# Two attention blocks on one core: narrower moment weights, paired denominators, products of zeros in planned gaps, and a retuned plan

## The chip, the cores and the metric

The kernel runs on one core of one Trainium2 chip. The metric is the device time of one execution in microseconds (us), taken over several executions, of which the median is used. TensorE (PE in the profile) multiplies matrices and writes PSUM, VectorE (DVE) and ScalarE (ACT) copy and transform, GpSimd (POOL) sets constants, SyncE (SP) and ScalarE's queue issue transfers (DMAs).

## The reference

Two independent blocks read inputs of 2048 rows by 640, with 32 heads of 20 columns each. Block A is softmax attention, block B is linear attention; their outputs stand side by side.

```python
# A, per head of 20 columns
scores = einsum("bhqd,bhkd->bhqk", q, k) * (Dh ** -0.5)
p = softmax(scores, axis=-1)
o = einsum("bhqk,bhkd->bhqd", p, v)          # then @ wo
# B, per head
phi = lambda t: where(t > 0, t + 1, exp(t)) + 1e-6
pq, pk = phi(q), phi(k)
kv = einsum("bhsd,bhse->bhde", pk, v)
z = einsum("bhsd->bhd", pk)
num = einsum("bhqd,bhde->bhqe", pq, kv)
den = einsum("bhqd,bhd->bhq", pq, z)[..., None] + 1e-6
o = num / den                                # then @ wo
```

## The kernel before, in words

Rows are cut into 16 tiles of 128 and into 4 chunks of 512 (`NQC`, index `tc` or `qc`). Both blocks are worked at once on the one core.

**Block A.** Scores are small for these inputs, so the exponential is replaced by a polynomial of second order in q and k (a guard, `t_guard`, measures whether that is allowed, and otherwise a general path runs). For each key tile, `t_kv` projects K and V, and `t_feat` makes the products of pairs of key columns on VectorE (lines 1372 and 1377, 16 tiles each, into `f_big`). `t_T` (line 1389) sums features times values over all tiles: these are the **moments**. The weights are `Vp`, 32 columns a head of which 20 hold V, one holds ones and 11 hold zeros; four heads go into four column tiles of TensorE, the feature operand has 242 columns, and 16 steps of 32 matmuls add up in four PSUM banks. `t_Tfin` turns the sums into the weight table `Tu`: small selecting matmuls and 24 products with a mask on VectorE (line 1464, the **spreads**), each of which frees the PSUM bank of a selecting matmul. Then come 22 **units** of queries: `t_psi` loads query rows by DMA into one of three slots of `f_big` and multiplies pairs on VectorE (line 1609), `t_pv` multiplies with `Tu` (24 matmuls, the **numerators** and their sums). `t_norm` brings the sums into another layout by DMA, inverts them, brings them back by two more DMAs and multiplies (line 1715), and `t_out` projects with `wo`; the last group's projection of 80 matmuls ends the kernel.

**Block B** (`b_tasks`, line 1810). Keys and values of a chunk are projected, `t_phi` applies phi (exponential on ScalarE, the relu at line 1780 and the sum at line 1803), and key-value products are added up over the four chunks (`kvmm`). For each chunk of queries `qden` projects q, applies phi, and forms the **denominators** (`dmm`, line 2019): five matmuls with 32 weight columns, `kvZ`, and 512 moving columns, into 32 PSUM partitions at `32*tc`. VectorE adds a constant (line 2029), a DMA folds the result into `dc`, VectorE inverts it (line 2038), four DMAs spread it into `Rb`, and `npost` (line 2047) multiplies phi(q) with it. `numout` projects with the combined matrix `Mp`.

**The order of the work.** Nothing is ordered by hand: `_Plan` (line 754) is a list planner that runs when the program is built. Every piece of work is a task with engines, a planned duration, a priority and the tasks that it waits for; a TensorE job also takes a PSUM bank. `step` picks the task that can start first in planned time, by priority among equals, and `run` issues its instructions. So planned durations (for a `job` columns / 2400 + 0.003 us for each entry of `cols`) and the priorities in `_C` fix the order of instructions of each engine, and each engine works through its queue in that order on the chip, with waits on semaphores where data are not there yet. `_WS`, `P1` to `P4` and `_C` are constants of that planner.

## Time and profile before

| | us |
|---|---|
| median of 5 runs | 308.49 |
| lowest, highest run | 306.91, 308.95 |
| the profiled execution | 309.22 |
| its span, first to last instruction | 307.4 |
| mean granted clock of TensorE | 0.983 |

Groups of part 5 of the page that belong to the parts that change (busy time is the union of a group's instructions, the mean is one instruction from start to end; matmuls overlap, so their means are longer than the distance from one to the next):

```profile
L172 PE MATMUL ps<-f_w,f_xT 128*64 128x320 bf16 x640 | 48.6, 307 | 3.1 <-DVE f_xT L1098 2.2
L1377 DVE TENSOR_TENSOR f_big<-f_big 128x3200 bf16<-128x3200 bf16 x16 | 29.1, 1820 | 3.1 <-ACT f_big L1094 3.1
L1609 DVE TENSOR_TENSOR f_big<-f_big 120x1536 bf16<-120x1536 bf16 (+3 forms) x66 | 67.0, 1015 | 4.2 <-DMA f_big<-f_Qd 2.7
```

Each line is: source line, engine, operation, output and inputs with their shapes, how often; then busy us and mean ns of one; then the idle time of that engine just ahead of these instructions and what ended most of it. All matmuls carry line 172, since one helper issues them.

### The profile page before, as it was taken

How to read it: one execution, taken by the hardware profiler on the slowest of the kernel's cores; microseconds unless marked ns; L12 is line 12 of the kernel's file. 1: busy time of each engine (PE TensorE's matmuls, PEld its weight loads, DVE VectorE, ACT ScalarE, POOL GpSimd, SP SyncE). 2: the span in 40 equal slices, each digit the busy share in tenths (PEclk: the TensorE clock that was granted, in tenths of full speed). 3: DMA queues.
4: the chain of work that ended last, by engine and by line, in shares of the span. 5: the costliest groups of instructions: out<-in, count | busy, mean ns of one | idle time of the engine just before them, and what ended most of it. 6: DMA issues, size and time to landing. Idle time of an engine off the chain costs nothing.

```text
span 307.4 us, 8859 instructions
## 1 busy us (share of the span) xinstructions
PE 289.7 (94%) x3807; PEld 193.0 (63%) x3807; DVE 252.3 (82%) x345; ACT 188.3 (61%) x386; POOL 11.5 (4%) x37
## 2 busy tenths in 40 slices
PE   5988999999999997999998899999999889999995
PEld 2766777778565763466666666557554446677873
DVE  6989989999939788977797988999878899994310
ACT  3668788899998772143544256586654475464563
POOL 7200000000000010000000000200000000000000
PEclk9899999999999999599999999999999999999999
DMA  7999565860130337058347736365989979455562
GB/s 250 315 187 188 95 99 92 288 141 9 29 103 20 100 101 220 25 138 209 103 100 220 156 105 179 106 168 117 286 209 185 204 214 229 152 162 176 178 195 94
DMA packets 58745, 47.24 MB, mean 154 GB/s; under 512 B 22994, under 2 KB 57619, under 8 KB 58699
## 3 DMA queue, kind: packets, MB, share of 16 engines
q1 hardware_dynamic: 52443, 38.60, 50.3%
q10 hardware_dynamic: 6256, 8.00, 8.8%
q8 instruction: 32, 0.52, 0.7%
q14 instruction: 14, 0.11, 0.2%
HBM read 30.65 MB, written 11.25 MB: 136 GB/s over the span
## 4 chain that ended last, share of the span: by engine, by line
PE 66%; DVE 13%; DMA 11%; ACT 5%; issue 1%; ACTq 1%; SPq 0%; POOL 0%; DVEq 0%; POOLq 0%
PE ps L172 66%; DMA f_big<-f_Qd 7%; DVE f_big L1609 3%; DVE f_Tu L1464 2%; DMA f_Nd<-f_Rc 2%; DMA f_w<-f_Nd 2%; DVE f_big L1377 2%; DVE f_big L1372 2%; ACT f_big L1094 1%; ACT f_ex L1784 1%; ACT f_pk L1094 1%; ACT f_Ks L1094 1%; DVE f_r L1780 1%; DVE f_pk L1803 1%; ACTq L1689 1%
## 5 line engine op out<-in xcount | busy, mean ns | idle before, releaser
L1609 DVE TENSOR_TENSOR f_big<-f_big 120x1536 bf16<-120x1536 bf16 (+3 forms) x66 | 67.0, 1015 | 4.2 <-DMA f_big<-f_Qd 2.7
L172 PE MATMUL ps<-f_big,f_Tu 120*64 120x512 bf16 (+3 forms) x484 | 54.7, 373 | 3.2 <-DVE f_big L1609 1.6
L172 PE MATMUL ps<-f_w,f_xT 128*64 128x320 bf16 x640 | 48.6, 307 | 3.1 <-DVE f_xT L1098 2.2
L172 PE MATMUL ps<-f_wB,f_xB 128*64 128x320 bf16 x640 | 47.7, 300 | 1.6 <-ACT f_ex L1784 1.0
L172 PEld LDWEIGHTS ps<-f_w,f_xT 128*64 128x64 bf16 x640 | 35.4, 112 | 14.5 <-DVE f_xT L1098 2.3
L172 PEld LDWEIGHTS ps<-f_big,f_Tu 120*64 120x64 bf16 (+1 forms) x484 | 27.5, 109 | 25.7 <-DVE f_big L1609 3.0
L172 PEld LDWEIGHTS ps<-f_wB,f_xB 128*64 128x64 bf16 x640 | 35.8, 110 | 11.0 <-ACT f_ex L1784 1.3
L1094 ACT COPY f_xT<-ps 126x512 f32<-126x512 f32 (+3 forms) x29 | 15.6, 540 | 35.4 <-PE ps L172 32.9
L1094 ACT CAST f_pk<-ps 128x320 bf16<-128x320 f32 (+4 forms) x63 | 25.6, 416 | 10.7 <-PE ps L172 10.3
L1377 DVE TENSOR_TENSOR f_big<-f_big 128x3200 bf16<-128x3200 bf16 x16 | 29.1, 1820 | 3.1 <-ACT f_big L1094 3.1
L1784 ACT ACTIVATE f_ex<-ps 128x320 f32<-128x320 f32 (+1 forms) x52 | 25.2, 500 | 9.7 <-PE ps L172 3.4
L1372 DVE TENSOR_TENSOR f_big<-f_big,f_Ks 128x3200 bf16<-128x3200 bf16 x16 | 29.1, 1820 | 0.0
L172 PE MATMUL ps<-f_xT,f_w 128*64 128x512 bf16 (+3 forms) x240 | 28.1, 404 | 0.0
L172 PE MATMUL ps<-f_wo,f_w 128*64 128x320 bf16 x320 | 23.7, 300 | 0.8 <-ACT f_xT L1094 0.6
L172 PE MATMUL ps<-f_xB,f_wB 128*64 128x512 bf16 x200 | 23.7, 379 | 0.1
L1622 ACT ACTIVATE f_Dq<-f_big 120x512 bf16<-120x512 bf16 (+1 forms) x22 | 13.7, 621 | 14.7 <-DMA f_big<-f_Qd 10.1
L1780 DVE TENSOR_SCALAR f_r<-ps 128x320 f32<-128x320 f32 x32 | 15.1, 488 | 8.4 <-ACT f_ex L1784 7.6
L172 PEld LDWEIGHTS ps<-f_wo,f_w 128*64 128x64 bf16 x320 | 17.5, 110 | 6.5 <-issue 1.4
L172 PEld LDWEIGHTS ps<-f_xT,f_w 128*64 128x64 bf16 (+3 forms) x240 | 12.1, 112 | 12.9 <-issue 4.0
L1094 ACT CAST f_qk<-ps 120x512 bf16<-120x512 f32 (+1 forms) x21 | 12.1, 585 | 12.8 <-PE ps L172 12.7
L1094 ACT CAST f_big<-ps 128x320 bf16<-128x320 f32 (+1 forms) x31 | 13.5, 436 | 8.5 <-PE ps L172 8.4
L172 PEld LDWEIGHTS ps<-f_xB,f_wB 128*64 128x64 bf16 x200 | 11.9, 110 | 9.5 <-ACT f_ex L1784 0.3
(131 smaller groups left out, 369.4 us busy)
## 6 DMA issues: line engine op xcount, KB each, us to landing
f_big<-f_Qd SPq DMA_DIRECT2D x20, 480.0 KB, 5.3
f_big<-f_Qd SPq DMA_DIRECT2D x20, 240.0 KB, 6.5
f_Qd<-f_qk SPq DMA_DIRECT2D x20, 120.0 KB, 1.9
f_Rbc<-f_Nd ACTq DMA_DIRECT2D x3, 720.0 KB
f_w<-f_Nd ACTq DMA_DIRECT2D x4, 480.0 KB
out_dram<-f_pk SPq DMA_DIRECT2D x12, 160.0 KB, 2.1
f_wB<-in_B_wqkv_dram SPq DMA_DIRECT2D x2, 800.0 KB
out_dram<-f_w SPq DMA_DIRECT2D x8, 160.0 KB, 2.8
```

The lines of the kernel that those rows point to most:

```text
L172: lambda e: e.matmul(out, lhsT, rhs, start=start, stop=stop, tile_position=tp, skip_group_check=sgc),
L1094: return self.sch.op("act", lambda e: e.copy(out, in_), reads=reads, writes=writes)
L1372: sch.op("dve", lambda e: e.tensor_tensor(F[:, :, 122:222].rearrange("p h (d a) -> p h d a", a=20), k0.unsqueeze(2).broadcast_to([128, 32, ...
L1377: sch.op("dve", lambda e: e.tensor_tensor(F[:, :, 22:122].rearrange("p h (d a) -> p h d a", a=20), k0.unsqueeze(2).broadcast_to([128, 32, ...
L1464: sch.op("dve", lambda e: e.tensor_tensor(dst.rearrange("p b (v h) -> p b v h", h=nh), src.rearrange("p b (h v) -> p b v h", h=nh), mask.u ...
L1609: sch.op("dve", lambda e: e.tensor_tensor(sl[:, o:o + n, :], sl[:, a:a + 1, :].broadcast_to([120, n, N]), sl[:, b:b + n, :], op=ALU.mult), ...
L1622: sch.op("act", lambda e: e.activation(self.Dq[0:120, dq, 0:N], sl[:, 0, :], AF.Square), reads=(k0,), writes=(("Dq", dq),))
L1689: fn3.append(lambda e, n=n, o=o, i=i, m=m, w=w: e.dma_start(self.Rbc[rb][0:120, i:i + m, 0:w], bass.AP(t.tensor, t.offset + o, [[0, 20], [ ...
L1780: sch.op("dve", lambda e: e.tensor_scalar(r1, ps[:, j.bank, 0:n], 0.0, 1e-6, op0=ALU.max, op1=ALU.add), reads=(("ps", j.bank),), writes=(( ...
L1784: sch.op("act", lambda e: e.activation(ex, ps[:, j.bank, 0:n], AF.Exp), reads=(("ps", j.bank),), writes=(("ex", k, h),))
L1803: sch.op("dve", lambda e: e.scalar_tensor_tensor(dst, self.ex[:, k, 0:m], 1.0, self.r1[:, k, 0:m], op0=ALU.min, op1=ALU.add), reads=tuple( ...
```

## The change

Five things are edited. The moments load 21 of the 32 weight columns in all steps but the first, which still writes the zeros of the other partitions. B's denominators are formed for two chunks in one job, alternately in two column tiles, and the constant's addition and the reciprocal work on both chunks at once. `run` of the planner gets a `fill`: where a TensorE job that takes one bank starts, in planned time, later than TensorE and the bank are free, three quarters of the gap (less 0.2 us) are filled with products of a 128 by 128 block of zeros into that bank. Planned durations of three kinds of job are altered (moments, key-value products, denominators), and the writes of `Tu` are made to wait, in the plan, for two weight permutations whose input they overwrite. All but three of the constants in `_C` have new values. The arithmetic of the result is the same.

```diff
--- before.py
+++ after.py
@@ -765,6 +765,7 @@
         self.open = 0
         self.mode = None
         self.now = 0.0
+        self.fill = None
 
     def add(self, task, deps=()):
         task.seq = self.seq
@@ -872,6 +873,7 @@
         t.start = s0
         if t.acq is not None:
             bk = []
+            x = None
             for pool in t.acq:
                 if pool == "sel2":
                     for x in sorted(self.banks["sel"])[:2]:
@@ -899,6 +901,10 @@
                 tok.remove(x)
                 bk.append(x[1])
             t.bank = bk[0] if len(bk) == 1 else tuple(bk)
+            if e == "pe" and self.fill and len(bk) == 1 and s0 > 12.0:
+                n = int(0.75 * (s0 - max(self.free[e], x[0]) - 0.2) / 0.22)
+                if n > 0:
+                    self.fill(t.bank, n)
         dur = t.durs[t.engs.index(e)]
         if e == "pe" and t.mode is not None:
             if t.mode != self.mode:
@@ -944,8 +950,9 @@
 P3 = (0.0, 0.4)
 P4 = (0.0, 0.6)
 _WS = 176
-_C = dict(q=0.62, qs=0.04, ks=0.0, kd=-0.005, bk=8.07, bks=0.0, bq=-3.62, bo=0.169, out=1.37, pv=0.0, fe=4.51,
-          psi=7.74, r=-3.6, f=-1.2, nm=0.91, op=4.0, kv=3.3, npo=0.1, bqs=0.0013, bd=0.0, bn=3.56)
+_C = dict(q=1.22, qs=0.002, ks=-0.005, kd=0.002, bk=8.14, bks=0.02, bq=-1.65, bo=0.169, out=0.65, pv=0.05,
+          fe=5.19, psi=8.0, r=-3.73, f=-3.51, nm=-0.06, op=5.55, kv=5.2, npo=0.04, bqs=0.0013, bd=0.0,
+          bn=3.21)
 
 
 class _Fast:
@@ -1395,12 +1402,13 @@
             for g in range(N_GRP):
                 for i in range(4):
                     h = 4 * g + i
-                    sch.mm(ps[32 * i:32 * i + 32, g // 2, 256 * (g % 2):256 * (g % 2) + 242], self.Vp[:, s2, h, :],
+                    w = 21 if t else 32
+                    sch.mm(ps[32 * i:32 * i + w, g // 2, 256 * (g % 2):256 * (g % 2) + 242], self.Vp[:, s2, h, 0:w],
                            self.F[:, s, h, 0:242], start=(t == 0 and g % 2 == 0), stop=(t == self.NT - 1),
                            reads=(("Vp", s2, h // 16), "Vp0", ("F1", s)) + keys,
                            writes=(("ps", g // 2),), tp=(0, 32 * i), inc=(g == N_GRP - 1 and i == 3), sgc=True)
             yield
-        return self.job(mms, [293] * N_GRP, deps, prio=0.5, pool=None)
+        return self.job(mms, [245] * N_GRP, deps, prio=0.5, pool=None)
 
     def t_Tfin(self, last):
 
@@ -1481,7 +1489,7 @@
                     sch.barrier(("dve",), ("w0r", "w0B"))
                 spread(self.Tu[0:m, x, 0:4, :], ps[0:m, j.bank, 0:504].rearrange("p (b w) -> p b w", b=4),
                        self.M6[0:m], m)
-            done.append(self.dve(0.68, post, (j,), prio=0.2, rel=(("aux", j),)))
+            done.append(self.dve(0.68, post, (j, self.ew[0], self.ewB[0]), prio=0.2, rel=(("aux", j),)))
         for q in range(6):
             def mms(b, q=q):
                 for y in range(2):
@@ -1501,7 +1509,7 @@
                 for y in range(2):
                     m = 120 if q + y else 123
                     spread(self.Tu[0:m, 2 * q + y, 4:6, :], v[0:m, 2 * y:2 * y + 2, :], self.M6[0:m], m)
-            done.append(self.dve(0.84, post, (j,), prio=0.2, rel=(("aux", j),)))
+            done.append(self.dve(0.84, post, (j, self.ew[0], self.ewB[0]), prio=0.2, rel=(("aux", j),)))
         done = [plan.add(_Task("none", 0.0, lambda t: None), done)]
         self.ones = []
         for s in range(self.NS):
@@ -1811,7 +1819,7 @@
         sch, ps = self.sch, self.ps
         NQC = self.NQC
         kvprev = (start,)
-        kvlast, kvx, dcl = [], {}, {}
+        kvlast, kvx, dcl = [], {}, []
         PB, BK = _C["bq"], _C["bk"]
 
         def va1(_):
@@ -1855,7 +1863,7 @@
                                     writes=(("ps", b),), inc=(c == cs[-1] and tl == 3), sgc=True)
                             one = False
                     yield
-                j = self.job(kvmm, [290] * (4 * len(cs)), ks + vs, prio=_C["kv"])
+                j = self.job(kvmm, [185] * (4 * len(cs)), ks + vs, prio=_C["kv"])
                 kvprev.append(j)
 
                 def kvpost(_, j=j, cs=cs, tc=tc):
@@ -2014,41 +2022,49 @@
                 qj.append(j)
                 qs.append(self.t_phi([j], 512, pqT[:, c, :], ("pqT", tc, c), fr, fw, eps=False))
             qall[tc] = self.plan.add(_Task("none", 0.0, lambda t: None), qj)
-            pr = slice(32 * tc, 32 * tc + 32)
+            return qs
+
+        def den(k, qs):
+
+            tcs = (2 * k, 2 * k + 1)
+            pr = slice(64 * k, 64 * k + 64)
 
             def dmm(b):
                 for c in range(N_DC):
-                    sch.mm(ps[pr, b, :], self.kvZ[:, c, :], pqT[:, c, :], start=(c == 0), stop=(c == N_DC - 1),
-                           reads=("kvZ", ("pqT", tc, c)), writes=(("ps", b),), tp=(0, 32 * tc),
-                           inc=(c == N_DC - 1))
+                    for tc in tcs:
+                        sch.mm(ps[32 * tc:32 * tc + 32, b, :], self.kvZ[:, c, :], pqs[tc][:, c, :], start=(c == 0),
+                               stop=(c == N_DC - 1), reads=("kvZ", ("pqT", tc, c)), writes=(("ps", b),), tp=(0, 32 * tc),
+                               inc=(c == N_DC - 1 and tc % 2 == 1), sgc=True)
                 yield
-            j = self.job(dmm, [590] * 5, qs + [zf], prio=_C["bd"])
-
-            def dpost(_, j=j):
+            j = self.job(dmm, [540] * 5, qs + [zf], prio=_C["bd"])
+
+            def dpost(_):
                 sch.barrier(("dve",), tuple(("mask", c) for c in range(N_DC)) + ("mask0",))
                 sch.op("dve", lambda e: e.tensor_scalar(self.dn[pr, :], ps[pr, j.bank, :], self.cn[pr, 0:1], 1e-6,
                                                         op0=ALU.add, op1=ALU.add),
-                       reads=(("ps", j.bank), "cn"), writes=(("dn", tc),))
-            e1 = self.dve(0.62, dpost, (j, cn), prio=1.0, rel=(("aux", j),))
-            dc = self.dc[:, tc % 2, :]
-            m1 = self.spd([lambda e: e.dma_start(dc, self.dn[pr, :].rearrange("h (j q) -> h j q", j=4))],
-                          (e1, dcl.get(tc - 2)), (("dn", tc),), (("dc", tc % 2),), prio=0.5, q="act", lat=6.0)
+                       reads=(("ps", j.bank), "cn"), writes=(("dn", k),))
+            e1 = self.dve(0.7, dpost, (j, cn), prio=1.0, rel=(("aux", j),))
+            m1 = self.spd([lambda e, tc=tc: e.dma_start(
+                self.dc[:, tc % 2, :], self.dn[32 * tc:32 * tc + 32, :].rearrange("h (j q) -> h j q", j=4)) for tc in tcs],
+                [e1] + dcl[-2:], (("dn", k),), ("dc",), prio=0.5, q="act", lat=4.5)
 
             def rc(_):
-                sch.op("dve", lambda e: e.reciprocal(dc, dc), reads=(("dc", tc % 2),), writes=(("dc", tc % 2),))
-            e2 = self.dve(1.1, rc, (m1,), prio=0.9)
-            k = tc % 2
-            m2 = self.spd([lambda e, i=i: e.dma_start(self.Rb[32 * i:32 * i + 32, k, :].rearrange("h (j q) -> h j q", j=4), dc)
-                           for i in range(4)],
-                          (e2, bar, rbprev.get(tc - 2)), (("dc", tc % 2),), (("Rb", k),), prio=0.5, lat=5.0)
-            dcl[tc] = m2
-
-            def npost(_):
-                sch.op("dve", lambda e: e.scalar_tensor_tensor(
-                    pqT, pqT, 1e-6, self.Rb[:, k, :].unsqueeze(1).broadcast_to([128, N_DC, 512]), op0=ALU.add,
-                    op1=ALU.mult), reads=(("Rb", k),), writes=tuple(("pqT", tc, c) for c in range(N_DC)))
-            rbprev[tc] = self.dve(2.9, npost, (m2,), prio=_C["npo"])
-            return rbprev[tc]
+                sch.op("dve", lambda e: e.reciprocal(self.dc[:], self.dc[:]), reads=("dc",), writes=("dc",))
+            e2 = self.dve(1.9, rc, (m1,), prio=0.9)
+            res = []
+            for tc in tcs:
+                m2 = self.spd([lambda e, i=i, tc=tc: e.dma_start(
+                    self.Rb[32 * i:32 * i + 32, tc % 2, :].rearrange("h (j q) -> h j q", j=4), self.dc[:, tc % 2, :])
+                    for i in range(4)], (e2, bar, rbprev.get(tc - 2)), ("dc",), (("Rb", tc % 2),), prio=0.5, lat=5.0)
+                dcl.append(m2)
+
+                def npost(_, tc=tc):
+                    sch.op("dve", lambda e: e.scalar_tensor_tensor(
+                        pqs[tc], pqs[tc], 1e-6, self.Rb[:, tc % 2, :].unsqueeze(1).broadcast_to([128, N_DC, 512]),
+                        op0=ALU.add, op1=ALU.mult), reads=(("Rb", tc % 2),), writes=tuple(("pqT", tc, c) for c in range(N_DC)))
+                rbprev[tc] = self.dve(2.9, npost, (m2,), prio=_C["npo"])
+                res.append(rbprev[tc])
+            return res
 
         def numout(tc, nm):
             pqT = pqs[tc]
@@ -2075,11 +2091,11 @@
                     self.out[128 * t:128 * (t + 1), D_MODEL:2 * D_MODEL], self.stB[sg - 4])],
                     evs, (("st", sg, 0), ("st", sg, 1)), (("bout", t),), lat=6.5)
 
-        held = []
+        nms = []
+        for k in range(NQC // 2):
+            nms += den(k, qden(2 * k) + qden(2 * k + 1))
         for tc in range(NQC):
-            held.append((tc, qden(tc)))
-        for x in held:
-            numout(*x)
+            numout(tc, nms[tc])
 
 
 
@@ -2142,6 +2158,13 @@
             self.ex_[tc] = plan.add(_Task("none", 0.0, lambda t: None), (self.ext[tc][0], self.ext[tc][3]))
         xn_free = [self.ex_[0], self.ex_[1]]
         cdone = self.cdone = self.mid_consts()
+
+        def fill(b, n):
+
+            mv = self.zt[:].unsqueeze(1).broadcast_to([128, 4, 128])
+            for _ in range(n):
+                sch.mm(ps[:, b, :], self.zt[:], mv, start=True, stop=True, reads=("zt",), writes=(("ps", b),), sgc=True)
+        plan.fill = fill
 
         TP, kns, feats, vqs = [], [], [], []
         for t in range(NT):
```

## The prediction

> **What bounds the kernel now.** I read the page first (parts 1, 2 and 4), then the busy time by stretches of 10 us, then TensorE's own waits, then TensorE's timeline around the places that the diff touches. The page gives the frame.
>
> ```profile
> span 307.4 us, 8859 instructions
> PE 289.7 (94%) x3807; PEld 193.0 (63%) x3807; DVE 252.3 (82%) x345; ACT 188.3 (61%) x386; POOL 11.5 (4%) x37
> PEclk9899999999999999599999999999999999999999
> PE 66%; DVE 13%; DMA 11%; ACT 5%; issue 1%; ACTq 1%; SPq 0%; POOL 0%; DVEq 0%; POOLq 0%
> ```
>
> TensorE (PE) is busy 289.7 of 307.4 us, idle 17.7. It is the bound, and a microsecond of its queue is worth about a microsecond if the next thing it waits for is ready. One slice has half clock. The chain of waits agrees: 66% on TensorE. The stretches show where the 17.7 us are, and where VectorE (DVE) is nearly as full.
>
> ```profile
> 20.00:30.00 10.00, 8.96 (x164) 6.60 (x160) 8.32 (x10) 8.19 (x16) 0.00 (x0) 1.00 0.97 199
> 30.00:80.00 50.00, 49.56 (x890) 38.67 (x888) 47.66 (x49) 43.69 (x88) 0.00 (x0) 1.00 0.53 115
> 80.00:110.00 30.00, 30.00 (x431) 18.86 (x428) 23.15 (x26) 25.60 (x45) 0.00 (x0) 1.00 0.25 72
> 126.00:127.00 1.00, 1.00 (x8) 0.36 (x4) 0.93 (x3) 0.00 (x0) 0.00 (x0) 0.50 0.00 0
> 150.00:180.00 30.00, 27.57 (x376) 19.79 (x374) 25.56 (x41) 13.94 (x34) 0.00 (x0) 1.00 0.62 161
> 240.00:250.00 10.00, 7.85 (x80) 4.11 (x78) 8.90 (x12) 5.61 (x12) 0.00 (x0) 1.00 0.77 199
> ```
>
> Columns: stretch, PE, weight loads, DVE, ACT, POOL, clock, DMA. Idle of TensorE: about 5.5 us in the first 30, nearly nothing from 30 to 110 (the moments), some 2 around 120, 5.4 between 150 and 250 (the numerators), 3.8 after its last matmul. From 30 to 80 VectorE is at 95% too; from 80 to 110 only at 77%. In one-microsecond stretches the clock is 0.50 from 123.7 to 130.1. The timeline gives the prices of what is changed, and the end of the kernel:
>
> ```profile
> 55.43 1.01 PE L172 MATMUL ps<-f_big,f_Vp 128*32 128x242 bf16 x32
> 56.37 2.91 PE L172 MATMUL ps<-f_w,f_xT 128*64 128x320 bf16 x40
> ...
> 220.40 1.25 PE L172 MATMUL ps<-f_pq,f_kvZ 128*32 128x512 bf16 x5
> 221.58 2.57 PE L172 MATMUL ps<-f_big,f_Tu 123*64 123x512 bf16 x22
> ...
> 275.87 2.54 PE L172 MATMUL ps<-f_big,f_Tu 123*64 123x512 bf16 x22
> 278.25 0.38 PE L172 MATMUL ps<-f_Dq,f_Tu 120*64 120x512 bf16 x2
> ...
> 297.99 5.62 PE L172 MATMUL ps<-f_wo,f_w 128*64 128x320 bf16 x80 [0.17 <-DVE f_w L1715]
> ```
>
> Start to start, a moments step takes 0.94 us and a denominator job 1.18. After the last numerator ends (278.6), TensorE fills 19.4 us with projections while that numerator is copied, inverted and scattered by DMAs; the last 80 matmuls wait only 0.17 us for it.
>
> **What the Trainium skill says.** "TensorE: Matmul & The Clock Gate", section "LDWEIGHTS (loading the stationary operand)": the load's time goes by its columns, columns / 1.2 ns. The trace: 32 loads of 32 columns took 0.74 us, 23.1 ns each, a little under its 26.7. The same page, "What's actually happening": the clock is halved after an idle window and comes back after about 3.4 us of activity. The trace has one such stretch, 6.4 us, though TensorE never stood for more than 0.28 us at a time there; it was thinly used. "TensorEngine Tiling (Array Packing)", "Theoretical Speedup": operands of 64 columns or less run up to 2 at once in column tiles. The trace has it: ten 512-column matmuls of 64 columns go in 1.08 us, 0.216 a pair. The same page, "Key Properties": changing the tiling mode drains the array; no row of this trace isolates that cost.
>
> **The change part by part.** *Moments.* Each of 16 steps has 8 groups of four (load, matmul) pairs; 0.94/8 = 117 ns a group. Loads alone, from the page: 4 x 26.7 = 107 ns with 32 columns, 70 with 21 (estimate). Streaming alone, from the 320-column pairs (0.140 us a pair): 242/320 x 0.140 = 0.106. With 21 columns streaming is the floor: 8 x 0.106 = 0.85 us. 15 steps change (the first keeps 32), so the gain is between 0 and 15 x 0.09 = 1.4; I take 1.3.
>
> *Denominators.* Before, 4 x 1.18 = 4.72 us. After, two jobs of five pairs, 2 x 5 x 0.216 = 2.16 (if they overlapped not at all: 4.72). I take -2.5; bounds -2.6 and 0. VectorE gains too: four additions of 744 ns become two, 1.5 us, and the reciprocal stays about the same (four of 916 ns against two of twice the columns). Against it: the chain dn, DMA, reciprocal, DMA, product now waits for both chunks. In the new order of instructions 22 us of TensorE work stand between the second pair of denominators and the first numerators of chunk 2, and the old landings were 5.8 and 6.8 us (f_wB<-f_dc, f_dc<-f_dn), so I cost it at nothing; if the cover failed, about 3 us.
>
> *Products of zeros.* The new order holds 11: 3 early, 1 ahead of a numerator, 1 near the end, 6 ahead of the last 80 matmuls. One is 512 columns, 0.216 us at full clock. The early 3 fall where TensorE idles anyway (1.04 us between 20 and 30). The last 6 fill a gap that the planner thinks at least 0.2 + 6 x 0.22/0.75 = 1.96 us long. I don't see that gap: from the last numerator to the last 80 the new order has 290 projection matmuls at 0.070, 20.3 us, and some 0.6 of small work, against a chain that took 19.4. So 8 are pure addition, 1.7 us, and four switches of mode at the planner's 0.105 add 0.4: +2.1; bounds 0 (all in real gaps) and +2.8. None of the 11 stands in the stretch of half clock: there the matmuls wait for a free bank, and the fill begins only once the bank is free. So that stays.
>
> *Planner figures alone.* The two jobs of B's key-value products (40 matmuls) were planned at 20 x 0.124 = 2.48 us; they took 1.59, from 190.53 to 192.12, and the new figure gives 1.60. With the retuned constants and the two added dependencies of the Tu writes this moves the whole order. Up to the last moments step the new order has 80 fewer matmuls of B's keys and values (80 x 0.070 = 5.6) and 60 fewer of A's queries (6 x 1.08 = 6.5); with the moments' 1.3 that is 13.4 us less for TensorE, so its last moments step could start at 110.3 - 13.4 = 97. VectorE up to the last feature product: 96.6 us of work in the first 110.2, less 4 relus (0.41 each), one 640-wide sum (0.74), four copies (0.4) and the two guard reductions: about 91.5. With the 4.4 us it loses at the start between 0 and 30 and the 4.7% it idles from 30 to 80, it ends at about 98 to 99. So in the moments both engines are now full; TensorE waits 1.5 us more for features, and 12 us of its work move to where VectorE has time. From the Tu spreads on, VectorE has the same work as before in a stretch some 10 us longer. What it left late, part of the 5.4 us between 150 and 250, should shrink; bounds -4 and +2, as loads there land only after 10.6 to 12 us (chain of waits, 219 to 246) and don't care for VectorE. I take -2.4. After them the first thing late is again the numerators' slots.
>
> Sum: -1.3 - 2.5 + 2.1 + 1.5 - 2.4 = -2.6. The profiled execution took 309.22 us (span 307.4 and 1.8 around it): 306.6. The median shown is 0.73 lower, so 305.9.
>
> **The rivals.** *A, slower: the moments go at VectorE's pace.* If VectorE's idle time up to the last product stays at 110.2 - 96.6 = 13.6 us, since features wait for ACT copies that wait for TensorE, the last step starts at 91.5 + 13.6 = 105 and TensorE has nothing ready: 8 us of waits in place of 1.5, so 305.9 + 6.5 = 312.4. It turns slower by over 0.5% once the last step starts later than about 101.5. For it: VectorE at 95% from 30 to 80. Against: most of that idle (6.9 us) lies in 80 to 110, where TensorE alone was full, and at the start. *B, no change: the later stalls stay.* They are waits for loads, not for VectorE; with -2.4 gone, 308.3. For it: those 10 to 12 us landings. *C, more than forecast:* the fills fall in real gaps (-2.1) and the moments add no wait (-1.5): 302.3. For it: the planner's figures now agree with the trace for several kinds of job. That the change doesn't do what it says applies to its fills alone, and is in the sum.
>
> **How the numbers follow.** Forecast 0.48 (302.8 to 307.5), A 0.24, B 0.16, C 0.12. About 0.5% (1.5 us) is what a measurement of this kernel can tell from no change. Faster: forecast and C, 0.60; same: B, 0.16; slower: A, 0.24. The range goes from 301.5 to 311: it holds the forecast, B, most of C and half of A. The likeliest case's own range is the one given with its chance.
>
> **What would show it.** Moments step at 0.85 us start to start; the pair of denominators at 1.1; the last moments step at 97 to 101; one stretch of clock 0.50 of about 6 us after the spreads; last 80 matmuls after six zero products with no wait in between; TensorE idle in the numerators below 4 us. Wrong if TensorE idles before moments steps for over 5 us, or the half clock comes twice.

## The result and the profile after

The changed kernel takes 310.29 us (median of 42 runs, 307.3 to 312.76), the kernel before beside it 308.41 (79 runs, 306.16 to 311.75): a ratio of 1.0063, 95% interval 1.0048 to 1.0077. A ratio leaves out executions that took over 1.5% longer than the fastest of the same kernel; medians and extremes hold all. The prediction was 305.9 and faster; the change made the kernel slower by 1.9 us. The profiled execution took 309.8 us with a span of 307.9, against 309.22 and 307.4: these two differ by 0.6 us only, so the stretches below show where time went in one execution each and don't add up to the 1.9.

The page of the changed kernel, its head and the shares of its chain of waits:

```profile
span 307.9 us, 8876 instructions
PE 289.2 (94%) x3818; PEld 192.9 (63%) x3818; DVE 250.6 (81%) x340; ACT 188.0 (61%) x387; POOL 11.5 (4%) x37
PEclk9799999999999998999999999999999979999999
PE 70%; DVE 13%; DMA 9%; ACT 3%; issue 1%; SPq 1%; ACTq 0%; POOL 0%; POOLq 0%; DVEq 0%
```

TensorE is busy 0.5 us less than before and idle 18.7 us in place of 17.7. Of its clock (the digits of `PEclk`, tenths of full speed in 40 slices of the span), the 5 of before (the slice from 123) has become an 8 (from 115), but a 7 has appeared further on (from 246). Busy time by stretches of the span (columns: stretch, length, PE, weight loads, DVE, ACT, POOL, clock, DMA share, GB/s) shows where the idle time went:

```profile
30.00:110.00 80.00, 78.72 (x1296) 56.33 (x1292) 74.91 (x86) 69.21 (x132) 0.99 (x2) 1.00 0.43 98
230.00:262.00 32.00, 26.73 (x288) 15.91 (x286) 25.05 (x24) 15.55 (x33) 0.00 (x0) 0.95 0.73 185
```

TensorE's idle time, length less busy time, stretch by stretch:

| stretch, us | before | after |
|---|---|---|
| 0 to 30 | 5.48 | 4.27 |
| 30 to 110 (moments) | 0.44 | 1.28 |
| 110 to 130 (spreads) | 2.21 | 1.75 |
| 130 to 230 | 3.33 | 1.95 |
| 230 to 262 | 2.25 | 5.27 |
| 262 to the end | 3.95 | 4.20 |

Everything up to 230 improved by 2.2 us in sum, and 3.0 were lost between 230 and 262. TensorE's timeline there (start, length from first start to last end, then the instructions; in brackets the idle time ahead of them and what ended it):

```profile
234.94 3.56 PE L172 MATMUL ps<-f_wo,f_w 128*64 128x320 bf16 x50
241.09 2.56 PE L172 MATMUL ps<-f_big,f_Tu 123*64 123x512 bf16 x22 [2.59 <-DVE f_big L1617]
...
251.30 1.54 PE L172 MATMUL ps<-f_pk,f_pq 128*64 128x320 bf16 x10 [2.69 <-DVE f_pq L2062]
252.64 1.98 PE L172 MATMUL ps<-f_xB,f_wB 128*64 128x512 bf16 x10
```

Two waits, 2.59 us for products of query rows and 2.69 for B's phi(q) times its inverted denominators; then the clock is halved for 3.4 us (250.7 to 254.1): ten 320-column matmuls take 1.54 us, elsewhere 0.85 to 0.87, ten of 512 columns 1.98, elsewhere 1.25. VectorE's timeline of the same stretch gives the reason for both:

```profile
232.91 0.74 DVE L1702 RECIPROCAL f_Rc<-f_Rc 96x96 f32<-96x96 f32 x1
236.22 1.75 DVE L2052 RECIPROCAL f_dc<-f_dc 128x256 f32<-128x256 f32 x1 [2.57 <-DMA f_dc<-f_dn]
237.89 3.15 DVE L1617 TENSOR_TENSOR f_big<-f_big 120x2048 bf16<-120x2048 bf16 x3
...
248.42 2.83 DVE L2062 SCALAR_TENSOR_TENSOR f_pq<-f_pq,f_wB 128x2560 bf16<-128x2560 bf16 x1 [2.86 <-DMA f_wB<-f_dc]
```

VectorE stands still for 2.57 us at the first pair's reciprocal, whose operand comes by DMA. Behind it in the same queue are the products for TensorE's next numerators (line 1617, unit 17), whose query rows had landed by 233.4 (ScalarE squared them then). They start only at 237.89, and TensorE waits at 241.09. The second standstill is at B's product, line 2062. In the kernel before, VectorE came to the first two reciprocals 11 us after ScalarE's queue issued their DMAs (239.76), and did not stand there:

```profile
250.85 1.76 DVE L2038 RECIPROCAL f_dc<-f_dc 128x128 f32<-128x128 f32 x2
```

The two waits share the loss differently from one execution to the next. In those of e1 (the changed kernel without the zeros) and e2 (with 32 weight columns throughout), both below and otherwise in the same order, the first wait was 2.47 and 3.42 us, the half clock came right behind it (the 22 matmuls took 4.09 and 3.96 us), and the second wait was 0.22 and 0.40.

### The profile page after: what moved, and what is told of

Read it like the earlier page. It is cut to its first block, busy times and chain, and to the rows that moved or that the text cites. A ratio compares the mean times of both kernels' runs of the same rounds, so it can differ in the third digit from the quotient of the medians.

```text
span 307.9 us, 8876 instructions
## 1 busy us (share of the span) xinstructions
PE 289.2 (94%) x3818; PEld 192.9 (63%) x3818; DVE 250.6 (81%) x340; ACT 188.0 (61%) x387; POOL 11.5 (4%) x37
## 4 chain that ended last, share of the span: by engine, by line
PE 70%; DVE 13%; DMA 9%; ACT 3%; issue 1%; SPq 1%; ACTq 0%; POOL 0%; POOLq 0%; DVEq 0%
PE ps L172 70%; DMA f_big<-f_Qd 3%; DMA f_dc<-f_dn 3%; DMA f_wB<-f_dc 3%; DVE f_Tu L1472 2%; DVE f_big L1384 2%; DVE f_big L1379 2%; DVE f_big L1617 1%; DVE f_pq L2062 1%; DVE f_pq L1284 1%; ACT f_ex L1792 1%; SPq L2056 1%; DVE f_dc L2052 1%; DVE f_dn L1286 1%; ACT f_pk L1101 1%
## 5 line engine op out<-in xcount | busy, mean ns | idle before, releaser
L172 PE MATMUL ps<-f_big,f_Tu 120*64 120x512 bf16 (+4 forms) x484 | 54.6, 373 | 3.4 <-DVE f_big L1617 2.6
L172 PEld LDWEIGHTS ps<-f_big,f_Tu 120*64 120x64 bf16 (+2 forms) x484 | 26.9, 109 | 25.4 <-DVE f_big L1617 3.3
L172 PEld LDWEIGHTS ps<-f_wB,f_xB 128*64 128x64 bf16 x640 | 36.5, 110 | 8.3 <-issue 1.1
L1792 ACT ACTIVATE f_ex<-ps 128x320 f32<-128x320 f32 (+1 forms) x52 | 25.6, 499 | 10.4 <-PE ps L172 8.6
L172 PE MATMUL ps<-f_xT,f_w 128*64 128x512 bf16 (+2 forms) x240 | 26.5, 389 | 0.0
L172 PE MATMUL ps<-f_xB,f_wB 128*64 128x512 bf16 x200 | 24.4, 387 | 0.0
L1101 ACT CAST f_big<-ps 128x320 bf16<-128x320 f32 (+1 forms) x33 | 14.2, 435 | 9.6 <-PE ps L172 9.3
L172 PEld LDWEIGHTS ps<-f_xT,f_w 128*64 128x64 bf16 (+2 forms) x240 | 11.9, 108 | 11.1 <-issue 1.0
L1797 ACT ACTIVATE f_r<-ps 128x512 f32<-128x512 f32 x20 | 11.9, 596 | 10.4 <-PE ps L172 8.5
```

The lines of the kernel that those rows point to most:

```text
L172: lambda e: e.matmul(out, lhsT, rhs, start=start, stop=stop, tile_position=tp, skip_group_check=sgc),
L1101: return self.sch.op("act", lambda e: e.copy(out, in_), reads=reads, writes=writes)
L1792: sch.op("act", lambda e: e.activation(ex, ps[:, j.bank, 0:n], AF.Exp), reads=(("ps", j.bank),), writes=(("ex", k, h),))
L1797: sch.op("act", lambda e: e.activation(r1, ps[:, j.bank, 0:n], AF.Relu), **rw)
```

## The experiments

Ratios are to the kernel before, run on the same chip in the same period. The intervals don't hold what differs between chips: one order of instructions, run twice on two chips (e10 and e15 below), gave 1.0095 and 1.0036, another (e5 and e13) 0.9928 and 0.9949.

**Zeros and weight columns taken back.** e1 is the changed kernel with `plan.fill = None`, e2 has `w = 32` in all steps.

> The changed kernel with the same plan, but the 11 products of zeros are not issued; all else is in the same order. Theory: the eight after 190 us stand on TensorE's path (1.40 us ahead of the last 80 matmuls, 0.46 ahead of a numerator, 0.3 near the end), so the median falls from 310.3 by 1.5 to 2.5 us, to about 308.3, and the last 80 matmuls start about 2 us earlier. Rival: they keep the clock up or fill waits that are there anyway; then the time stays within 0.5 us of 310.3 or rises, and a further stretch of clock 0.50 shows.

> The changed kernel with 32 weight columns in all moments steps, the plan unaltered. Theory: the width of the weights does not set the pace of a step, which stays at 0.94 us start to start, and the time stays within 0.5 us of 310.3. Rival (the prediction's reading): loads of 21 columns are faster and the gain is only hidden by waits for features; then steps take longer than those of the changed kernel, and the time rises by up to 1.4 us, to 311.7.

e1: 309.24 us, ratio 1.0034 (1.0009 to 1.0058). The zeros cost about 0.9 us (1.0063 less 1.0034, times 308; the intervals just overlap), so at most half of the loss: 1.0 us of it stays without them. e2: 309.97, ratio 1.0065 (1.0032 to 1.0098), the same as the changed kernel within the intervals: 21 or 32 weight columns make no difference that shows.

**What a moments step costs.** The widths are changed in pairs of steps. e8 leaves out part of the computation: columns of V or of the features in eight of the 16 steps.

```diff
-                    w = 21 if t else 32
+                    w, nf = {3: (32, 242), 4: (32, 242), 5: (8, 242), 6: (8, 242), 7: (21, 121), 8: (21, 121),
+                             9: (32, 121), 10: (32, 121), 11: (21, 32), 12: (21, 32)}.get(t, (21 if t else 32, 242))
...
```

> The changed kernel with other shapes in some moments steps (so the sums of those steps leave out parts of V or of the features): steps 3, 4: 32 weight columns and 242 moving columns; 5, 6: 8 and 242; 7, 8: 21 and 121; 9, 10: 32 and 121; 11, 12: 21 and 32; the others 21 and 242. Start to start, now 0.94 us. Theory: a pair of load and matmul costs 29.4 ns whatever the widths, so all steps stay within 0.05 us of 0.94. Rival S (streaming bounds): steps with 121 moving columns fall to 0.45 to 0.55 us. Rival L (loads bound): step time goes with the weight columns, 8 columns well below 21.

TensorE's timeline of that kernel, two steps and what follows each (128*8 is 128 rows by 8 weight columns; 128x242 the moving operand):

```profile
44.17 1.00 PE L172 MATMUL ps<-f_big,f_Vp 128*8 128x242 bf16 x32
45.11 0.60 PE L172 MATMUL ps<-f_w,f_xT 128*64 128x320 bf16 x6
...
59.89 0.61 PE L172 MATMUL ps<-f_big,f_Vp 128*21 128x121 bf16 x32
60.43 0.46 PE L172 MATMUL ps<-f_w,f_xT 128*64 128x320 bf16 x4
```

Start to start a step takes 0.94 us with 8 weight columns, as with 21 and 32, and 0.54 with half the moving columns (0.53 to 0.54 with 32 weight columns too); with 32 moving columns it took 0.30. Per group of four matmuls that is 117, 67 and 37 ns: 0.41 ns a moving column between the first two, and some 17 ns that don't go by columns (some 24 at 32 columns). My theory, that each pair of load and matmul has a price of its own whatever the widths, fell; the rival, that the streaming of the moving columns sets the pace, stands. The Trainium skill ("TensorE: Matmul & The Clock Gate", "Measured speedup vs the span model") gives a pack of tiles the time of one matmul plus some 4 ns for each further tile; that is 12 ns for four tiles, as an estimate, where e8 has 17.

**Is the second wait a matter of where B's first projection stands?** e3 makes chunk 0's projection wait, in the plan, for the second pair's denominators (`hold` in its list); e4 is e3 without zeros.

> The changed kernel, with one edit to the plan: B's projections of chunk 0 may be planned only after the second pair of denominators, so that the first of them no longer stands in TensorE's queue ahead of the last ten query matmuls and a numerator. Theory: the 2.7 us wait for phi(q) times the inverse and the stretch of half clock after it (about 1.4 us lost) go, and the median falls by 3 to 4 us, to about 306.8. Rival: the queue then waits at the next numerator or at the slots' loads instead, the gain is below 1 us, and a wait of over 2 us shows within 10 us of the old place.

> Both edits at once: the held projection and no products of zeros. Theory: the two costs stand in different places of TensorE's queue and add up: 310.3 - 3.5 - 2 = about 304.8, faster than both kernels. Rival: the end of the kernel is then set by the last group's chain of DMAs (its product ended 0.26 us before TensorE came to the zeros), so that only one of the two gains is kept, about 306.8.

e3: 309.91, ratio 1.0025 (1.0001 to 1.0049); e4: 308.86, 1.002 (0.9993 to 1.0048). The wait ahead of B's projection went, but the wait ahead of the numerators grew to 3.54 us, and its 22 matmuls then took 4.90 us in place of 2.56: the loss had another place to go.

**Is it the reciprocal's place?** e5, without zeros, lets the reciprocal of the first pair wait, in the plan, for unit 17's products.

```diff
-            e2 = self.dve(1.9, rc, (m1,), prio=0.9)
+            e2 = self.dve(1.9, rc, (m1, self.pd[17] if k == 0 else None), prio=0.9)
```

> The changed kernel without products of zeros, and with one more dependency in the plan: the reciprocal of the first pair of denominators waits for the pair products of unit 17, so that on VectorE it stands behind them and not ahead of them. (The planner then also places B's first projections later.) Theory: in the changed kernel the reciprocal stands in VectorE's queue while its DMA takes 9.4 us where 4.5 were planned; the products behind it, whose rows landed at 233.4, start only at 237.9, and TensorE waits 2.6 us for them, with half clock after it in some executions. With the order turned round that wait falls below 0.8 us, VectorE's wait for f_dc<-f_dn falls below 1 us, and against the kernel without zeros (309.2) the median falls by 2.5 to 3.5 us, to about 306.3. Rival: the rows of the unit are what is late, as loads take 7 to 12 us there; then the wait of about 2.5 us stays and the time stays within 1 us of 309.2.

305.98 us, ratio 0.9928 (0.9902 to 0.9953): faster than both kernels. In VectorE's timeline of e5 the products now come first and the reciprocal stands 0.69 us:

```profile
233.87 3.21 DVE L1617 TENSOR_TENSOR f_big<-f_big 120x2048 bf16<-120x2048 bf16 x3 [0.54 <-DMA f_big<-f_Qd]
237.76 1.75 DVE L2053 RECIPROCAL f_dc<-f_dc 128x256 f32<-128x256 f32 x1 [0.69 <-DMA f_dc<-f_dn]
```

Between 230 and 262 TensorE is busy 31.32 of 32 us (26.73 in the changed kernel). I took this for proof that the place of one instruction was the loss. But a new dependency lets the planner place everything behind it anew, and the next runs show that more had moved.

**The halves of the change alone.** e6 is the kernel before with the new constants, the new durations of moments and key-value products, and the `Tu` dependencies; e7 is the kernel before with the paired denominators only, the planned landings of their DMAs among them.

> The kernel before with only the retuned constants, the planner's new figures and the two added dependencies: 32 weight columns, denominators chunk by chunk, no products of zeros. Theory: the new order by itself costs nothing (VectorE is fuller in the moments, TensorE idles no more), the reciprocals stand late enough in VectorE's queue, and the median is within 1 us of 308.2. Rival A: the new order itself is what is slow, with TensorE waiting for features; then the last moments step starts later than 99 us and the median is over 309.7. Rival B: the order is better, as predicted: 306.5 or less.

> The kernel before with only the paired denominators; constants and all other figures as before. TensorE has 2.4 us less work. Theory: the pair's reciprocal stands again in VectorE's queue ahead of a unit's products, its DMA lands late, TensorE waits 2 us or more before a numerator between 235 and 255, and the gain is spent: the median is within 1 us of 308.2. Rival: the harm needs the retuned order; then there is no such wait and the median falls by 2 us or more, to 306.2.

e6: 309.94, ratio 1.0053 (1.0032 to 1.0074). e7: 310.98, ratio 1.0073 (1.0044 to 1.0102). Each loses alone. e6 has no large wait, but many small ones between 230 and 262 (3.84 us idle, before 2.25) and 1.47 idle in the moments (before 0.44); I did not trace them further. Its last moments step starts at 97.35, so it isn't the prediction's rival A, which had it at 105. e7 has the pattern of the changed kernel: the pair's reciprocal stands 2.94 us for its DMA ahead of products, and TensorE waits 1.69 for those.

**The same dependency elsewhere, and on the whole change.** e9 is e7 with e5's dependency, e10 the whole change, zeros too, with it.

> Kernel before with the pairs of denominators alone, and the one dependency more: the first pair's reciprocal waits for unit 17's products. Theory (the pairs hurt because the shared reciprocal waits for its DMA at the head of VectorE's queue, ahead of products whose rows have landed): the wait of 1.69 us ahead of the numerators near 244 is gone or under 0.5, the reciprocal follows its wait by under 1 us, and the kernel is at 306.0 to 307.5 against 308.3 for before. Rival (the pairs hurt through their late second half, where VectorE ends later and the last 80 matmuls wait for it; the dependency only moves the order): still 308.5 or more, with the last 80 matmuls waiting 1 us or more. The new order also puts the first pair some 40 us earlier, so a miss with neither wait would mean that the rest of the order decides.

> The whole change, products of zeros among it, with that one dependency. The planner now puts 20 products of zeros ahead of the last 80 matmuls, where it saw 6, and one ahead of B's last 80. Theory: the two waits of 2.6 and 2.7 us and the half clock between 251 and 254 are gone (-5 or so), and the 20 zeros (4.3 us) take the place of a wait of 2.76 us there and add about 1.5 to 2: 307 to 308.5, 1.5 to 2.5 slower than the same kernel without zeros. Rival (zeros keep the clock up and cost nothing, being in a real gap): equal to the kernel without zeros, 306.

e9: 312.0, ratio 1.0128 (1.0087 to 1.0169), a miss. The wait it aimed at is gone and the first pair's denominators stand where they stood (226.08 us, in e7 226.34), but the order behind them changed and other waits came (1.11 us ahead of an output projection, 1.06 ahead of numerators, 1.35 ahead of the last 80 matmuls). Which of them costs the time was not tried. e10: 310.35, ratio 1.0095 (1.0062 to 1.0128): the two waits and the half clock are gone as expected, and the planner had put 20 zeros ahead of the last 80 matmuls; the time was above the range I gave.

**One exchange and nothing else.** e5 changed more than one place. So in e11 only two entries of VectorE's queue are exchanged after planning (the reciprocal is issued right behind unit 17's products; all other engines keep their order); e12 does that to e3.

```diff
-                sch.op("dve", lambda e: e.reciprocal(self.dc[:], self.dc[:]), reads=("dc",), writes=("dc",))
+                def op():
+                    sch.op("dve", lambda e: e.reciprocal(self.dc[:], self.dc[:]), reads=("dc",), writes=("dc",))
+                if k == 0:
+                    self.kept.append(op)
+                else:
+                    op()
...
             mul(1, 0, 1, 3, (k0, k2), (("sl", s, "C"), k2))
+            if self.kept:
+                self.kept.pop()()
```

> The changed kernel with two instructions' places exchanged and nothing else: the first pair's reciprocal is written behind unit 17's three products on VectorE; every other engine has the same order. Theory (two stalls share one chain: dn, DMA, reciprocal, DMA, product, first B projection): the wait of 2.59 us ahead of the numerator near 241 is gone, so TensorE reaches B's first projection 2.6 us earlier; but its inputs come 0 to 1 us later than before, so the wait there grows from 2.69 to between 5 and 6.5 us and the time stays, 309.8 to 311.5 (ratio 1.004 to 1.010). Rival (the reciprocal's place alone is the loss): the first wait goes, the second grows by under 1 us, and the time falls by 2 to 3, to 307.3 to 308.3 (ratio 0.997 to 1.000).

> The kernel with B's first projection held behind the second pair's denominators, and the same exchange of places on VectorE and nothing else. Theory (each of the two is enough to keep the loss, so they have to go together): the wait of 3.54 us ahead of the numerator near 243 and its half clock (4.90 for 22 matmuls, 2.54 at full clock) both go, and no wait over 1 us takes their place between 235 and 262; of the 5.9 us at that place 2 or more may come back as waits for the last group's chain at the end, so 304.5 to 307 (ratio 0.987 to 0.996, against 1.0025 without the exchange). Rival (the chain of loads behind sets the pace, and the waits only move): the time stays at 308.5 or more, and waits of the same sum stand later.

e11: 313.16, ratio 1.0155 (1.0108 to 1.0203). The direction is the theory's, the size beyond it. TensorE's timeline of e11:

```profile
247.34 0.61 PE L172 MATMUL ps<-f_Dq,f_GW 120*32 120x512 bf16 x6
254.14 1.54 PE L172 MATMUL ps<-f_pk,f_pq 128*64 128x320 bf16 x10 [6.19 <-DVE f_pq L2069]
255.48 2.34 PE L172 MATMUL ps<-f_xB,f_wB 128*64 128x512 bf16 x10
257.61 3.29 PE L172 MATMUL ps<-f_big,f_Tu 123*62 123x512 bf16 x22
```

The first wait has shrunk to nothing and the second has grown from 2.69 to 6.19 us, with a longer stretch of half clock behind it (6.8 us in place of 3.4). The reciprocal itself now runs 2.8 us later (239.01 in place of 236.22), and B's product with it (251.26 in place of 248.42). e12: 311.44, ratio 1.01 (1.0053 to 1.0148): my theory, that both waits go if both places are mended, fell. VectorE's timeline of e12 shows why:

```profile
250.84 2.83 DVE L2070 SCALAR_TENSOR_TENSOR f_pq<-f_pq,f_wB 128x2560 bf16<-128x2560 bf16 x1 [6.58 <-DMA f_wB<-f_dc]
253.58 1.48 DVE L1813 SCALAR_TENSOR_TENSOR f_xB<-f_ex,f_r 128x512 bf16<-128x512 f32 x2
...
257.71 0.69 DVE L1813 SCALAR_TENSOR_TENSOR f_xB<-f_ex,f_r 128x512 bf16<-128x512 f32 x1
```

VectorE stands 6.58 us at B's product for its second DMA, and behind it in the queue is phi of the last chunk's queries (line 1813), which the second pair's denominators need: TensorE waits 3.46 us there, for an exponential on ScalarE, whose queue had itself stood 5.94 us for line 1813, and 1.62 us for line 1813 itself. The queue is held by the same chain, one step further on. So it isn't the place of one instruction alone: my next theory was that the whole chain of the pair comes later than the plan has it, and that what is placed around it pays.

**The planned landing.** The planner counts 0.55 us to issue each DMA on ScalarE's queue and then `lat` until the data are there. The diff lowers `lat` of the sums' DMA from 6.0 to 4.5, an edit that the list of changes above does not name: planned 0.55 + 6.0 = 6.55 us before, where the trace of before has 6.8 from issue to landing (the last figure; the query counts the first two of the four DMAs):

```profile
f_dc<-f_dn ACTq DMA_DIRECT2D x2, 64.0 KB, 6.8
```

In the changed kernel it is 2 x 0.55 + 4.5 = 5.6 us from the first of the pair's two issues. That issue stood at 226.16 and the reciprocal could start at 236.22, 10.1 us later. Its chain of waits, from the second issue on:

```profile
226.82 9.38 DMA f_dc<-f_dn
236.22 1.76 DVE f_dc L2052
238.00 0.62 SPq L2056
...
239.95 8.44 DMA f_wB<-f_dc
248.42 2.84 DVE f_pq L2062
```

The second transfer is planned at 4 x 0.5 + 5.0 = 7.0 us from its first issue and took 10.4 (238.00 to 248.42). Over the two the chain is 7.9 us later than planned (4.5 and 3.4). e13 puts back 6.0 and nothing else, e14 sets both nearer the trace (8.0 and 7.0, so 9.1 and 9.0 planned), both without zeros; e15 is e13 with zeros; e16 gives e7 the figures of e14.

```diff
-                [e1] + dcl[-2:], (("dn", k),), ("dc",), prio=0.5, q="act", lat=4.5)
+                [e1] + dcl[-2:], (("dn", k),), ("dc",), prio=0.5, q="act", lat=8.0)
...
-                    for i in range(4)], (e2, bar, rbprev.get(tc - 2)), ("dc",), (("Rb", tc % 2),), prio=0.5, lat=5.0)
+                    for i in range(4)], (e2, bar, rbprev.get(tc - 2)), ("dc",), (("Rb", tc % 2),), prio=0.5, lat=7.0)
```

> The changed kernel without products of zeros, and one figure put back to what it was before the change: the planned landing of the sums' DMAs (dn to dc), 6.0 in place of 4.5. Theory (the planner believed the pair's sums would land early and put the reciprocal, B's products and B's first projection too early on three engines): the waits of 2.5 and 2.7 us in front of the numerator near 241 and of B's first projection go, and the time is that of the kernel with the reciprocal behind unit 17's products: ratio to before 0.989 to 0.996. Rival (the gain of that kernel was particular to its chip or its run): 1.000 or more.

> As the run before, with both landings of B's chain as the trace has them: 8.0 for dn to dc, 7.0 for dc to the multipliers. Theory: no wait for the reciprocal or for B's products; the same as the run before within 0.5%, since its order differs from it only after 262 (three products of the last group on VectorE, ScalarE's copies), 0.986 to 0.996. Rival: the later part gets worse, 1.000 or more, with a wait of more than 3 us before the last 80 matmuls.

> The changed kernel with the planned landing 6.0 in place of 4.5 and with its products of zeros (27, 20 of them ahead of the last 80 matmuls). Against the same without zeros on this chip: theory (they stand in a gap of 2.8 us and take 4.4; the six and one before add 1.3): 2 to 3 us slower, ratio to before 0.998 to 1.004. Rival (zeros cost more than their time, as two comparisons on different chips suggest): 4.5 to 5.5 slower, 1.006 to 1.012.

> The kernel before with the pairs alone and both landings as the trace has them (8.0 and 7.0). Theory (the pairs lose only by the early plan of their chain): better than with 4.5 and 5.0, which had 1.0073: 0.995 to 1.002. Rival (in this order the pairs bring other waits, as with the dependency alone, which had 1.0128): 1.007 or more, with waits of over 1 us ahead of an output projection or the last 80 matmuls.

All four ran on one chip, where before took 307.87:

| kernel | us | ratio | interval |
|---|---|---|---|
| e13, 6.0 and 5.0, no zeros | 306.47 | 0.9949 | 0.9926 to 0.9973 |
| e14, 8.0 and 7.0, no zeros | 302.77 | 0.9835 | 0.9783 to 0.9886 |
| e15, 6.0 and 5.0, with zeros | 309.48 | 1.0036 | 1.0017 to 1.0056 |
| e16, pairs alone, 8.0 and 7.0 | 309.53 | 1.0018 | 0.9986 to 1.0051 |

e13 has on every engine the order of e5, so what that dependency did, the one number does. Between 230 and 262 TensorE stands 1.35 us in e13, 5.27 in the changed kernel. Against e1 (1.0034) the number is worth 0.85% or 2.6 us; e1 ran on another chip, so the size is good only to the 0.2 to 0.6% by which one order differed between chips, but both chips that ran the order of e13 have it faster than before. e14 is the best kernel of the study, 5.1 us below before (six executions), and better than I expected; I had expected e13 and e14 equal. Between them only the end differs. VectorE's timeline of e13, near the end:

```profile
281.08 2.83 DVE L2062 SCALAR_TENSOR_TENSOR f_xB<-f_xB,f_wB 128x2560 bf16<-128x2560 bf16 x1 [3.56 <-DMA f_wB<-f_dc]
283.83 1.75 DVE L1723 TENSOR_TENSOR f_w<-f_xT,f_Rbc 120x1536 bf16<-120x1536 f32 x1
285.50 0.54 DVE L1702 RECIPROCAL f_Rc<-f_Rc 96x64 f32<-96x64 f32 x1
...
294.08 1.23 DVE L1723 TENSOR_TENSOR f_w<-f_xT,f_w 120x1024 bf16<-120x1024 f32 x1 [6.36 <-DMA f_w<-f_Nd]
```

and of e14:

```profile
273.95 0.55 DVE L1702 RECIPROCAL f_Rc<-f_Rc 96x64 f32<-96x64 f32 x1 [2.48 <-DMA f_Rc<-f_xT]
274.42 2.76 DVE L2062 SCALAR_TENSOR_TENSOR f_xB<-f_xB,f_wB 128x2560 bf16<-128x2560 bf16 x1
...
287.42 1.22 DVE L1723 TENSOR_TENSOR f_w<-f_xT,f_w 120x1024 bf16<-120x1024 f32 x1 [0.75 <-DMA f_w<-f_Nd]
```

With the later figures the planner puts block A's last reciprocal ahead of B's products, at 273.95 in place of 285.50, and the last product that the final 80 matmuls need comes at 287.42 in place of 294.08. In e13 those 80 wait 2.37 us; in e14 they follow without a wait, at 291.77. It is the same fault, at the second pair.

e15 is 3.0 us slower than e13 on the same chip: the planner's fill grows from 11 products of zeros to 31, most of them at the end. TensorE's timeline of e15:

```profile
293.00 4.49 PE L172 MATMUL ps<-f_zt 128*128 128x512 bf16 x20
297.42 5.62 PE L172 MATMUL ps<-f_wo,f_w 128*64 128x320 bf16 x80
```

Twenty zeros take 4.4 us where e13 waits 2.37 and e5 2.76, and the six and one ahead of B's last projection add some 1.3. So with the zeros the better figure brings no clear gain (1.0036 and 1.0095 in e15 and e10, against 1.0063).

e16 leaves the pairs alone open. Its ratio, 1.0018 where e7 on another chip had 1.0073, holds nine executions; the other six took 312.5 to 315.8 us, and none of the 51 of before took more than 310.4. The profiled execution is one of the six: VectorE no longer stands at the reciprocal, but TensorE waits 1.20 us ahead of an output projection and 2.97 ahead of numerators, waits like those that the rival named. In that order of work the landings alone don't explain the loss.

## Why the prediction was wrong, by its own steps

- **The step that failed**: "the chain dn, DMA, reciprocal, DMA, product now waits for both chunks ... so I cost it at nothing; if the cover failed, about 3 us". I looked at TensorE work ahead of the second pair's use, and took the old landings (5.8 and 6.8). I did not look at the first pair, at what stands behind its reciprocal in VectorE's queue, or at the figure 4.5 in the diff against the 6.8 in the trace of before. The runs showed in its place two waits, 5.3 us, and 1.4 us of half clock (0.67 and 0.73 over full clock). e13 puts the one figure at about 2.6 us, and e14, with both figures nearer the trace, lies 5.1 us below before; both were run without zeros. The cost of "if the cover failed", about 3 us, was of the right size: it was left out of the sum.
- **Moments, -1.3**: 0. A step stayed at 0.94. I scaled the 320-column pair (0.140 us, two tiles) by its columns to 106 ns. e8 has some 17 ns in each group of four tiles that columns don't shorten, and a group took 117 ns: streaming was the bound with 32 weight columns already.
- **Denominators, -2.5**: right. The first pair's job goes from 222.87 to 224.05, 1.18 us, so 2.4 for two in place of 4.72.
- **Zeros, +2.1**: about 0.9 (e1 against the changed kernel); more where the planner is told a later landing (3.0, e15 against e13, 31 zeros). The six ahead of the last 80 have no wait behind them, as said.
- **Waits in the moments, +1.5**: 0.84 (1.28 idle in place of 0.44). The last step started at 97.49, in the forecast's 97 to 101, in part by luck: the moments gave none of their 1.3, but TensorE idled 1.2 us less in the first 30 (4.27 in place of 5.48), which no term held. Rival A, the moments at VectorE's pace, did not occur: the kernel is slower, but for another reason.
- **Later waits, -2.4**: -1.4 up to 230, and +3.0 from 230 to 262, where the prediction said "after them the first thing late is again the numerators' slots". It was the query products behind a reciprocal, and B's own product.
- **Half clock**: I said that it would stay, and read it as 6.4 us; the clock of before has 6.8 (123.3 to 130.2). After the change it lasted 3.4 us (114.2 to 117.6), worth at most 1.7 us. That is not the change's doing: in e1, with the same order, it lasted 3.4 us, in e2 6.8. And it came a second time, which the prediction named as the sign that it was wrong.

## What to carry to other kernels

When a change merges two transfers into one chain, look at what is queued behind the instruction that waits for it on its own engine, not only at the time until its result is used; and where a planner orders the work, compare each latency that the change gives it with the landing in the trace (here 5.6 against 10.1 us) before anything else. "Issue the DMA early, do compute, wait on its semaphore late" (the Trainium skill, "DMA: Bandwidth & Descriptors", "Rules for kernel authors") paid here only where the plan knew how late: with the zeros left out, both figures set nearer the trace turned 0.3% slower (e1) into 1.65% faster (e14), on two chips. A gain from a new dependency is no proof of the reason for it: exchange the two instructions alone before you believe it.

## What the runs showed of the hardware that was not expected

- A DMA of 64 KB from one layout of the on-chip memory to another (`f_dc<-f_dn`) took 6.8 us from issue to landing before, 9.4 in the changed kernel and 9.5 in e5, while the DMA engines were busy for 0.87 of the time (before) and all of it (the other two), at 190 to 204 GB/s. The same DMA took 2.1 us in e7 for the second pair (from 265.8, the engines busy for 0.40 of the time) and 2.4 us for the last chunk of before (from 271.8, busy for 0.80). The Trainium skill ("DMA: Bandwidth & Descriptors", "Anatomy of one DMA") fits about 2.0 us plus bytes / 436e3 for another way of issuing, 2.15 us for 64 KB as an estimate: near the 2.1 and 2.4, far from the 9.4, and the measurement decides. So most of the landing near 230 us looks like queueing behind other transfers, for which the busy share is a rough sign only; whose, was not tried.
- The clock of TensorE halved at 250.7 after a wait of 2.69 us, but not after the 2.59 at 241, nor in e5 after 2.76 ahead of its last 80 matmuls (5.62 us). In the profiled execution of e13, with the order of e5, it halved after 2.37, and the last 80 took 7.30: that is why its profiled time (308.33) is above its median. The length of the wait doesn't decide it; how the wait falls on a grid agrees with all of these. In all 18 traces the clock changes only at whole multiples of 3.41 us from its first change. Cut on that grid, the changed kernel's stretch from 237.04 has TensorE busy for 0.43 of it, and full clock follows; that from 247.28 has 0.39, and half clock follows. In e13 one stretch holds the wait (busy 0.30), in e5 two share it (0.66 and 0.53). Between 30 and 300 us of the 18 traces, all 11 full-clock stretches with TensorE busy for 0.40 or less are followed by half clock, and none of the three between 0.43 and 0.58 is. After the spreads half clock follows at 0.59 to 0.67 too, which other places pass at full clock; what differs there stays open.
- A moments step took 0.94 us with 8, 21 and 32 weight columns alike: the load is hidden behind the streaming of 242 columns.
